# Attention products in plain float32 on tiles of the array, in place of split float32r products

## The chip, the cores and the metric

One Trainium2 chip, one of its cores. The metric is the device time of one launch in microseconds, as the median of several runs. The engines are TensorE (PE in the profile, with PEld for its weight loads), VectorE (DVE), ScalarE (ACT), GpSimd (POOL), and SyncE (SP), which issues nearly all DMA transfers of this kernel. Every engine, and SP's queue, works through its instructions in the order of the program.

## The reference, cut to what matters

Attention over 4 batches and 8 heads of size 64, with 512 local positions and 32 global ones; then two mixture stages on the 2176 tokens, which the change leaves alone.

```python
k_all = np.concatenate([k_g, k_l], axis=2)
v_all = np.concatenate([v_g, v_l], axis=2)
out_g = np.matmul(sm(scale * np.matmul(q_g, k_all.transpose(0, 1, 3, 2))), v_all)
s_ll = scale * np.matmul(q_l, k_l.transpose(0, 1, 3, 2))
s_ll = np.where(np.abs(pos[:, None] - pos[None, :]) <= 32, s_ll, -1000000000.0)
s_lg = scale * np.matmul(q_l, k_g.transpose(0, 1, 3, 2))
a_l = sm(np.concatenate([s_lg, s_ll], axis=-1))
out_l = np.matmul(a_l, np.concatenate([v_g, v_l], axis=2))
x = concatenate([out_g, out_l], axis=2) as 2176 x 512
x = _moe_ref(x, w_in, w_out)                 # relu, square, two products
return _moe2_ref(x, w_gate, w1, w2)          # Sinkhorn gate, 8 experts
```

`sm` is the softmax with 1e-9 added to its sum. A local query thus sees the 32 global keys and the local ones within 32 positions; a global query sees all 544 keys.

## The kernel before, in words

**Attention** comes first. Its work is cut into 16 items, one for each batch and pair of heads (two heads of 64 fill 128 partitions). An item has two local steps of 256 queries each (two tiles of 128 queries, for two heads), and after every second item comes a global step (32 queries of the four heads of two items, 128 rows in all): 40 steps, of which a cycle of five (four local, one global) covers two items. The loop (lines 856 to 927) is a software pipeline written out by hand: in iteration k each engine gets, in this order, the row minimum of step k-1 (`loc_least`, `glob_least`, on DVE; the scores are negated), the normalisation of step k-2 (`loc_normalise`: a reciprocal on DVE, four scalings on POOL), all evacuations that were noted since the last iteration (`evacuate_all`), the exponentials of step k-1 on ACT (`loc_exp`, `glob_exp`), and on TensorE the value products of step k-4 (`loc_values`, `glob_values`), the score products of step k (`loc_scores`, `glob_scores`), the transposes of the probabilities of step k-2 (`loc_transpose`, `glob_transpose`), and at the end of an item the transposes of the keys and queries of a coming item (`prep_qk`).

**Precision.** TensorE's fast form here is float32r, which rounds its operands. Each operand is kept as a half and a rest (hi and lo, both float32r), and each product is made of three: hi times hi, hi times lo, lo times hi (`split_terms`, line 199). So each value that goes from PSUM to SBUF is written twice: ACT casts it to hi (line 552 or 554), and DVE subtracts hi from the PSUM value to get lo (line 557 or 559). That holds for transposed keys (`trk` to `kt`), queries (`trq` to `q`), transposed probabilities (`pta` to `ah`/`al`, `ptb` to `bh`/`bl`), and the outputs (`pv` to `xh`/`xl`, one pair for each head). The values come by DMA to a staging tile, and POOL splits them (`split_pool`, lines 271 and 272).

**Products of a local step.** The scores (line 660) have a contraction of 64: the two heads stand on partitions 0 to 63 and 64 to 127, on two row tiles of the array, and each writes its own score tile: 12 products of 224 columns (128 local keys, 32 global ones, 32 on each side). The values (line 723) use the whole array: the stationary side holds the values of both heads, the moving side the probabilities of both heads (256 columns), so half of the result is not used; 12 products. Keys beside the tile and the global keys lie in the last 96 columns of `kt`, and the values that belong to them in `vb`; both are filled by DMAs inside SBUF (lines 606 to 609, 629 to 633).

**Products of a global step.** For the scores POOL writes the queries of four heads into a tile with zeros elsewhere (`glob_queries`, line 310); 12 products on the whole array (lines 746 and 747, 160 and 384 columns). The values (line 803) are 15 products of 256 columns, a quarter of whose result is used: `pick` takes the four blocks out with two ACT and two DVE instructions.

**What follows.** In the last six iterations the first products of the next stage (line 435) stand between the attention steps; side jobs (`step_side`) prepare its weights on ACT, DVE and POOL, one to three instructions for each iteration, more at the end. From then on order tables written out by hand set the work, and TensorE is kept busy to the end. The gate of the last stage (line 982) already uses plain float32 products, with four column tiles of 32.

Of the kernel before, what the change touches and what calls it, by code (L numbers as in the profile page):

```python
# [9 lines left out]
F32 = mybir.dt.float32  # L10
# [6 lines left out]
WINDOW = 32  # L17
# [188 lines left out]
def kernel(  # L206
# [240 lines left out]
    with ExitStack() as actx:  # L447
# [7 lines left out]
        rawqk, rawv = {}, {}  # L455
# [33 lines left out]
        def load_global(name, src, tag):  # L489
            graw[name] = ap2.tile([P, H * D], F32, tag=tag, name="graw")  # L490
# [7 lines left out]
        load_global("k", k_g, "ah")  # L498
        load_qk(1)
        load_v(0)  # L500
        load_global("v", v_g, "bh")
        load_global("q", q_g, "al")
# [3 lines left out]
        def warm(k):  # L506

            for _ in range(k):
                t = pss.tile([P, 384], F32, tag="pv", name="warm")
                nc.tensor.matmul(t, lhsT=bd[:, 0, 0:P], rhs=bd[:, 0, :], start=True, stop=True)  # L510
# [4 lines left out]
        nc.vector.memset(f32(bd[:, 0]), 0.0)  # L515
        nc.vector.memset(f32(bd[:, 1]), 0.0)
# [15 lines left out]
        for i in range(3):  # L532
            nc.gpsimd.memset(f32(KT[i][:, :, 0, 160:192]), 0.0)
            nc.gpsimd.memset(f32(KT[i][:, :, NQ - 1, 192:224]), 0.0)
            nc.gpsimd.memset(f32(VB[i][32:64, :, 0, :]), 0.0)
            nc.gpsimd.memset(f32(VB[i][64:96, :, NQ - 1, :]), 0.0)
        nc.gpsimd.memset(f32(gz), 0.0)
        for t in OG:
            nc.gpsimd.memset(t, 0.0)

        QT, VA = {}, {}
# [7 lines left out]
        def evacuate_all():  # L549
            for hi, lo, ps, scale in waiting:  # L550
                if scale == 1.0:
                    nc.scalar.copy(hi, ps)
                else:
                    nc.scalar.activation(out=hi, in_=ps, func=AF.Copy, scale=scale)
            for hi, lo, ps, scale in waiting:
                if scale == 1.0:
# [11 lines left out]
        def prep_qk(n):  # L568
# [11 lines left out]
            evacuate((kt[:, 0, :, 0:P], kt[:, 1, :, 0:P], trk, 1.0))  # L580
            if n < 3:
                evacuate((kt[:, 0, 1:, 160:192], kt[:, 1, 1:, 160:192], trk[:, :-1, P - WINDOW : P], 1.0))
                evacuate((kt[:, 0, :-1, 192:224], kt[:, 1, :-1, 192:224], trk[:, 1:, 0:WINDOW], 1.0))
            if n == 0:
                ps = turn_global("k", "pta")
                g = ps[:, p, b * SG : (b + 1) * SG].unsqueeze(1).to_broadcast([P, NQ, SG])
                evacuate((kt[:, 0, :, P : P + SG], kt[:, 1, :, P : P + SG], g, 1.0))
            q = ap2.tile([P, 2, NQ, P], F32R, tag="q", name="q")
            evacuate((q[:, 0], q[:, 1], trq, QSCALE))
            QT[n] = q  # L590
            if n == 0:
                evacuate((kg[:, 0], kg[:, 1], ps, 1.0))

        def prep_edges(n):
# [4 lines left out]
            keys = [f32(kg[:, x, p, b * SG : (b + 1) * SG]).unsqueeze(1).to_broadcast([P, NQ, SG]) for x in range(2)]  # L599
            if n < 3:  # L600
                nc.scalar.copy(kt[:, 0, :, P : P + SG], keys[0])
                nc.vector.tensor_copy(kt[:, 1, :, P : P + SG], keys[1])
# [14 lines left out]
        def prep_v(n):  # L617
# [3 lines left out]
            r = rawv.pop(n)  # L621
            if p % 2 == 0:
                VA[n // 2] = share.tile([P, 2, NQ, 2, P], F32R, tag=f"va{n // 2 % 2}", name="va")
            va = VA[n // 2][:, :, :, p % 2, :]
# [13 lines left out]


        kg = share.tile([P, 2, NP, P], F32R, tag="kg", name="kg")  # L640
        qg = ap1.tile([P, 2, NP, P], F32R, name="qg")
        vg = ap1.tile([P, 2, H * D], F32R, name="vg")
# [6 lines left out]
        def loc_scores(i, n, qp):  # L649
# [44 lines left out]
        def pt_tiles(i, *shapes):  # L694
            pt_t[i] = tuple(
                ap2.tile(shape, F32R, tag=x + y, name=x + y) for x, shape in zip("ab", shapes) for y in "hl"
            )
            return pt_t[i]

        def loc_transpose(i):  # L700
# [9 lines left out]
            ah, al, bh, bl = pt_tiles(i, [P, 2, 2 * P], [96, 2, 2 * P])  # L710
            evacuate((ah, al, pa.rearrange("p t j q -> p t (j q)"), 1.0), (bh, bl, pb[0:96].rearrange("p t j q -> p t (j q)"), 1.0))

        def loc_values(i, n, qp):
            b, p = items[n]
            ah, al, bh, bl = pt_t.pop(i)
            va, vb = VA[n // 2][:, :, :, p % 2, :], VB[n % 3]
            pv = pss.tile([P, 2, 2, P], F32, tag="pv", name="pv")
# [961 lines left out]
```

## Time and profile before

| what | value |
|---|---|
| runs shown | 1962.86, 1963.38, 1964.88 us; median 1963.38 us |
| profiled execution | 1959.21 us, of which the span of instructions is 1957.3 us |
| PE busy | 1928.7 us (99% of the span), 12482 products |
| DVE busy | 1443.9 us (74%) |
| ACT busy | 995.9 us (51%) |
| POOL busy | 581.4 us (30%) |
| mean granted TensorE clock | 0.997 |

A product's duration in the trace includes the time from its start until its last result is written; products follow one another at shorter distances than that, so their cost is read from the starts in the timeline. An engine's busy time in a stretch is the time that at least one of its instructions covers.

### The profile page before, as it was taken

The numbers are of one execution on the slowest core, as the hardware profiler recorded it, in microseconds if no ns is written. First come the engines' busy times: TensorE is split into PE (matmuls) and PEld (weight loads), VectorE is DVE, ScalarE is ACT, GpSimd is POOL, SyncE is SP. The second block draws the span as 40 slices with busy tenths as digits, with TensorE's granted clock in tenths as the row PEclk, the third lists the DMA queues.
The fourth block names the chain that finished last, engine by engine and source line by source line (L and its number), as shares of the span: only waits on it lengthen the run. The fifth ranks groups of instructions, "written<-read, shape, count | busy, mean of one in ns | idle before, by whom it ended". The sixth has DMA issues, their size and how long they took to land.

```text
span 1957.3 us, 34874 instructions
## 1 busy us (share of the span) xinstructions
PE 1928.7 (99%) x12482; PEld 1833.6 (94%) x12482; DVE 1443.9 (74%) x3075; ACT 995.9 (51%) x2325; POOL 581.4 (30%) x673
## 2 busy tenths in 40 slices
PE   9999999999999999999999999999999999999998
PEld 7888988989898899999999999999999999999998
DVE  7998575755359888888886776776777776767867
ACT  7988533323245555545554454454455454554543
POOL 6555431323126554555421101211103101111010
PEclk9999999999999999999999999999999999999999
DMA  7665220211016999998997667667676776676674
GB/s 163 139 144 133 66 65 22 65 44 49 28 32 224 308 302 301 306 301 299 311 329 269 211 224 250 214 237 244 206 260 213 248 249 236 207 258 225 208 267 141
DMA packets 359294, 391.34 MB, mean 200 GB/s; under 512 B 114256, under 2 KB 240208, under 8 KB 359120
## 3 DMA queue, kind: packets, MB, share of 16 engines
q1 hardware_dynamic: 359120, 389.10, 61.1%
q8 instruction: 99, 1.62, 0.3%
q14 instruction: 75, 0.61, 0.1%
HBM read 281.82 MB, written 96.73 MB: 193 GB/s over the span
## 4 chain that ended last, share of the span: by engine, by line
PE 90%; DVE 3%; ACT 2%; DMA 2%; SPq 1%; POOL 1%; issue 1%; DVEq 0%; POOLq 0%; ACTq 0%
PE z L1570 14%; PE a L1331 14%; PE y L1404 11%; PE h L435 10%; PE y L1078 9%; PE d L1570 7%; PE d L1331 7%; PE pa L1331 5%; PE b L1570 4%; PE b L1331 3%; PE pd L1331 2%; PE pb L1331 1%; PE pv L723 1%; ACT e L682 1%; DMA w2forms<-w 1%
## 5 line engine op out<-in xcount | busy, mean ns | idle before, releaser
L1202 POOL TENSOR_TENSOR w<-raw,w 128x256 fp32r<-128x256 f32 (+1 forms) x124 | 122.9, 1023 | 774.0 <-ACT w L1198 697.8
L1331 PE MATMUL a<-xh,w 128*128 128x384 f32 x1024 | 286.0, 335 | 0.0
L1543 ACT CAST xh<-wide 128x384 fp32r<-128x384 f32 x384 | 189.2, 512 | 112.9 <-PE d L1570 95.2
L1547 DVE TENSOR_TENSOR xl<-wide,xh 128x384 fp32r<-128x384 f32 x384 | 200.4, 549 | 24.7 <-ACT xh L1543 24.5
L1532 ACT COPY snaps<-a 128x384 f32<-128x384 f32 x128 | 61.3, 480 | 296.2 <-PE a L1331 224.8
L1404 PE MATMUL y<-w,xh 128*128 128x512 f32 x640 | 197.9, 390 | 0.7 <-ACT xh L1388 0.7
L1078 PE MATMUL y<-hid,w 128*128 128x384 f32 (+1 forms) x960 | 191.7, 356 | 0.0
L1584 DVE SCALAR_TENSOR_TENSOR acc<-z,prob,acc 128x256 f32<-128x256 f32 x366 | 162.0, 475 | 38.8 <-PE z L1570 38.7
L1331 PEld LDWEIGHTS a<-xh,w 128*128 128x128 f32 x1024 | 187.6, 188 | 0.0
L1078 PEld LDWEIGHTS y<-hid,w 128*128 128x128 f32 x960 | 171.9, 188 | 14.9
L435 PE MATMUL h<-xh,w 128*128 128x384 f32 (+1 forms) x640 | 182.6, 358 | 0.0
L1331 PE MATMUL a<-xl,w 128*128 128x384 f32 x512 | 171.2, 334 | 0.0
L1536 DVE TENSOR_TENSOR wide<-b,snaps 128x384 f32<-128x384 f32 x64 | 35.7, 557 | 157.9 <-PE b L1331 156.1
L1331 PE MATMUL d<-xh,w 128*128 128x384 f32 x512 | 150.5, 334 | 0.0
L441 ACT ACTIVATE r<-h 128x384 f32<-128x384 f32 (+1 forms) x76 | 40.4, 532 | 203.3 <-PE h L435 200.4
L1552 DVE TENSOR_TENSOR wide<-wide 128x384 f32<-128x384 f32 x256 | 138.8, 551 | 5.9 <-ACT wide L1540 0.8
L1404 PEld LDWEIGHTS y<-w,xh 128*128 128x128 f32 x640 | 119.2, 188 | 24.8 <-ACT xh L1388 1.1
L435 PEld LDWEIGHTS h<-xh,w 128*128 128x128 f32 x640 | 117.8, 188 | 13.3 <-issue 3.2
L1331 PE MATMUL pa<-xh,w 128*128 128x320 f32 x512 | 128.8, 310 | 1.0 <-ACT snaps L1366 0.6
L1404 PE MATMUL y<-w,xl 128*128 128x512 f32 x320 | 124.7, 390 | 0.9 <-DVE xl L1393 0.9
L1570 PE MATMUL z<-wf,xh 128*128 128x256 f32 x768 | 123.5, 283 | 0.0
L1540 ACT ACTIVATE wide<-wide 128x384 f32<-128x384 f32 x192 | 101.3, 528 | 33.0 <-DVE wide L1536 33.0
(255 smaller groups left out, 5073.4 us busy)
## 6 DMA issues: line engine op xcount, KB each, us to landing
raw<-in_moe_w_dram SPq DMA_DIRECT2D x128, 512.0 KB, 5.7
w<-w1forms SPq DMA_DIRECT2D x256, 256.0 KB, 4.9
w<-w2forms SPq DMA_DIRECT2D x256, 256.0 KB, 5.3
wf<-w2forms SPq DMA_DIRECT2D x192, 256.0 KB, 5.6
w1forms<-w SPq DMA_DIRECT2D x128, 256.0 KB, 4.2
w2forms<-w SPq DMA_DIRECT2D x192, 128.0 KB, 3.2
w2forms<-xl SPq DMA_DIRECT2D x64, 256.0 KB, 4.9
w2forms<-xh SPq DMA_DIRECT2D x64, 256.0 KB, 3.9
```

The lines of the kernel that those rows point to most:

```text
L435: nc.tensor.matmul(ps, lhsT=w, rhs=x, start=(k == 0), stop=(k == 3 * NC - 1))
L1078: nc.tensor.matmul(ps, lhsT=w, rhs=m, start=(f == 0 and x == 0), stop=(f == last and x == 2))
L1202: eng.tensor_tensor(out=lo, in0=src, in1=f32(hi), op=ALU.subtract)
L1331: nc.tensor.matmul(ps, lhsT=lhs, rhs=rhs, start=(first and t == 0), stop=(t == 5), skip_group_check=True)
L1404: nc.tensor.matmul(y[t0], lhsT=lhs, rhs=rhs, start=(t == 0), stop=(t == 3 * UF - 1))
L1532: act.copy(snap[{"1": "p1", "5": "p5" + q, "6": "u2" + q}[i]], bank(("d" if i == "5" else "a") + q)[:, 0:n])
L1540: act.activation(out=dst, in_=bank("a" + q)[:, 0:n] if name == "A21" else dst, func=AF.Relu)
L1543: act.copy(hidden_form(name, 0, int(q)), h[HOME[name]][int(q)])
L1547: dve.tensor_tensor(out=hidden_form(name, 1, q), in0=h[HOME[name]][q], in1=f32(hidden_form(name, 0, q)), op=sub)
L1552: dve.tensor_tensor(out=x, in0=x, in1=h[other][int(q)], op=op)
L1570: nc.tensor.matmul(ps, lhsT=lhs, rhs=rhs, start=(form in ("B11", "T1") and x == 0), stop=(x == 5), skip_group_check=True)
L1584: dve.scalar_tensor_tensor(out=dst, in0=width(t, src), scalar=pr, in1=dst, op0=mul, op1=add)
```

## The change

All products of attention become plain float32 products, each on a part of the array. There is one copy of each operand, no hi and lo. The scores of the two heads stay on two row tiles (four products a step); the values are made for each head on a column tile of 64 (eight products a step); the products of a global step are made for each of four blocks of 32 queries, the scores on a row half and a column tile of 32, the values on a column tile of 32. Evacuations are single copies, given to ACT ("a") or DVE ("v"); only the outputs still have hi and lo, since the next stage takes them so. The values go by DMA straight to `VA`, a ring of eight items, and POOL no longer splits them. `glob_queries` and the block tile `bd` are gone; `pick` is one instruction. `KT`, `VB`, `kg` and `vg` have half the bytes, and lie in the pool of attention rather than in the space shared with later weights. Cut to its core:

```diff
-        KT = [(ap1, share, share)[i].tile([P, 2, NQ, SEG], F32R, tag=f"kt{i}", name=f"kt{i}") for i in range(3)]
-
-        VB = [(ap1, share, share)[i].tile([P, 2, NQ, P], F32R, tag=f"vb{i}", name=f"vb{i}")[0:96] for i in range(3)]
-        bd = ap1.tile([P, 2, 384], F32R, name="bd")
-
-        gz = ap1.tile([P, 2, P], F32R, name="gz")
+        rawqk = {}
+
+        KT = [ap1.tile([P, NQ, SEG], F32, name=f"kt{i}") for i in range(3)]
+        VA = [share.tile([P, 2, NQ, 2, P], F32, tag=f"va{i}", name=f"va{i}") for i in range(2)]
+        VB = [ap1.tile([P, NQ, P], F32, name=f"vb{i}")[0:96] for i in range(3)]
+        kg, qg = (ap1.tile([P, NP, P], F32, name=n) for n in ("kg", "qg"))
+        vg = ap1.tile([P, H * D], F32, name="vg")
+        gz = ap1.tile([P, P], F32, name="gz")
...
+        def values_of(n):
+            return VA[n // 4 % 2][:, n // 2 % 2, :, n % 2, :]
+
         def load_v(n):
             if n >= len(items):
                 return
             b, p = items[n]
-            r = stage.tile([P, 2, NQ, 2, D], F32, tag="r1", name="rv")[:, 0]
-            load_pair(r, v_l, b, p)
-            rawv[n] = r
+            load_pair(values_of(n).rearrange("p t (h d) -> p t h d", h=2), v_l, b, p)
...
+            for eng, hi, lo, ps, scale in waiting:
+                if eng == "a":
+                    if scale == 1.0:
+                        nc.scalar.copy(hi, ps)
+                    else:
+                        nc.scalar.activation(out=hi, in_=ps, func=AF.Copy, scale=scale)
+            for eng, hi, lo, ps, scale in waiting:
+                if lo is not None:
                     nc.vector.tensor_tensor(out=lo, in0=ps, in1=f32(hi), op=ALU.subtract)
-                else:
-                    nc.vector.scalar_tensor_tensor(out=lo, in0=ps, scalar=scale, in1=f32(hi), op0=ALU.mult, op1=ALU.subtract)
+                elif eng == "v":
+                    if scale == 1.0:
+                        nc.vector.tensor_copy(hi, ps)
+                    else:
+                        nc.vector.tensor_scalar(out=hi, in0=ps, scalar1=scale, scalar2=None, op0=ALU.mult)
...
-            evacuate((kt[:, 0, :, 0:P], kt[:, 1, :, 0:P], trk, 1.0))
+            evacuate(("v", kt[:, :, 0:P], None, trk, 1.0))
...
-            q = ap2.tile([P, 2, NQ, P], F32R, tag="q", name="q")
-            evacuate((q[:, 0], q[:, 1], trq, QSCALE))
+                evacuate(("v", kt[:, :, P : P + SG], None, g, 1.0))
+            q = ap2.tile([P, NQ, P], F32, tag="q", name="q")
+            evacuate(("a" if n == 0 else "v", q, None, trq, QSCALE))
...
-                flat = f32(kt).rearrange("p x t k -> p (x t) k")
-                nc.sync.dma_start(out=flat[:, 1:, 160:192], in_=flat[:, :-1, P - WINDOW : P])
-                nc.sync.dma_start(out=flat[:, :-1, 192:224], in_=flat[:, 1:, 0:WINDOW])
-                for x in range(2):
-                    nc.sync.dma_start(out=f32(kt[:, x, :, P : P + SG]), in_=keys[x])
+                nc.sync.dma_start(out=kt[:, 1:, 160:192], in_=kt[:, :-1, P - WINDOW : P])
+                nc.sync.dma_start(out=kt[:, :-1, 192:224], in_=kt[:, 1:, 0:WINDOW])
+                nc.sync.dma_start(out=kt[:, :, P : P + SG], in_=keys)
...
-            split_pool(va[:, 0], va[:, 1], r.rearrange("p t h d -> p t (h d)"))
-            vb = VB[n % 3]
-
-            src, dst = (f32(x).rearrange("p x t d -> p (x t) d") for x in (va, vb))
-            nc.sync.dma_start(out=dst[32:64, 1:], in_=src[P - WINDOW : P, :-1])
-            nc.sync.dma_start(out=dst[64:96, :-1], in_=src[0:WINDOW, 1:])
-            for x in range(2):
-                g = vg[b * SG : (b + 1) * SG, x, p * P : (p + 1) * P]
-                nc.sync.dma_start(out=f32(vb[0:SG, x]), in_=f32(g).unsqueeze(1).to_broadcast([SG, NQ, P]))
+            va, vb = values_of(n), VB[n % 3]
+            nc.sync.dma_start(out=vb[32:64, 1:], in_=va[P - WINDOW : P, :-1])
+            nc.sync.dma_start(out=vb[64:96, :-1], in_=va[0:WINDOW, 1:])
+            g = vg[b * SG : (b + 1) * SG, p * P : (p + 1) * P]
+            nc.sync.dma_start(out=vb[0:SG], in_=g.unsqueeze(1).to_broadcast([SG, NQ, P]))
...
-                pairs = [split_terms(q[r, 0, qt], q[r, 1, qt], kt[r, 0, qt], kt[r, 1, qt]) for r in halves]
-                for x in range(3):
-                    for s, terms in zip(s_t[i], pairs):
-                        a, c = terms[x]
-                        nc.tensor.matmul(s[:, t, :], lhsT=a, rhs=c, start=(x == 0), stop=(x == 2))
+                for s, r in zip(s_t[i], halves):
+                    nc.tensor.matmul(s[:, t, :], lhsT=q[r, qt], rhs=kt[r, qt], start=True, stop=True)
...
-            ah, al, bh, bl = pt_tiles(i, [P, 2, 2 * P], [96, 2, 2 * P])
-            evacuate((ah, al, pa.rearrange("p t j q -> p t (j q)"), 1.0), (bh, bl, pb[0:96].rearrange("p t j q -> p t (j q)"), 1.0))
+            a, c = pt_tiles(i, [P, 2, 2, P], [96, 2, 2, P])
+            evacuate(("a", a, None, pa, 1.0), ("v", c, None, pb[0:96], 1.0))
...
-                terms = split_terms(va[:, 0, qt], va[:, 1, qt], ah[:, t], al[:, t])
-                terms += split_terms(vb[:, 0, qt], vb[:, 1, qt], bh[:, t], bl[:, t])
-                for x, (a, c) in enumerate(terms):
-                    nc.tensor.matmul(pv[:, t].rearrange("p j q -> p (j q)"), lhsT=a, rhs=c, start=(x == 0), stop=(x == 5))
+                for x, (v, e) in enumerate(zip(sources, pt)):
+                    for j, r in enumerate(halves):
+                        nc.tensor.matmul(pv[r, t], lhsT=v[:, qt, r], rhs=e[:, t, j], start=(x == 0), stop=(x == 1))
             c0 = b * SL + qp * 2 * P
-            part = lambda x, r: x[r, p, c0 : c0 + 2 * P].rearrange("p (t q) -> p t q", t=2)
-            evacuate(*((part(xh, r), part(xl, r), pv[r, :, j, :], 1.0) for j, r in enumerate(halves)))
-
-
-        def glob_queries(n):
-            b, p = items[n]
-            v = bd.rearrange("p x (i c) -> p x i c", c=192)
-            for j in range(2):
-                r = slice(j * D, (j + 1) * D)
-                for x in range(2):
-                    copy_pool(v[r, x, :, j * SG : (j + 1) * SG], f32(qg[r, x, p - 1 : p + 1, b * SG : (b + 1) * SG]))
+            part = lambda x: x[:, p, c0 : c0 + 2 * P].rearrange("p (t q) -> p t q", t=2)
+            evacuate(("a", part(xh), part(xl), pv, 1.0))
...
-            for x in range(2):
-                kt = KT[(n - 1 + x) % 3]
-                for y, (a, c) in enumerate(split_terms(bd[:, 0], bd[:, 1], kt[:, 0], kt[:, 1])):
-                    w = a[:, x * P : (x + 1) * P]
-                    first, last = (x == 0 and y == 0), (x == 1 and y == 2)
-                    nc.tensor.matmul(sa, lhsT=w, rhs=c[:, 0, 0 : P + SG], start=first, stop=last)
-                    nc.tensor.matmul(sb, lhsT=w, rhs=c[:, 1:NQ, 0:P], start=first, stop=last)
+            for x, (out, cols) in enumerate(((sa, lambda k: k[:, 0, 0 : P + SG]), (sb, lambda k: k[:, 1:NQ, 0:P]))):
+                for j, r in enumerate(halves):
+                    for y in range(2):
+                        g = slice((2 * j + y) * SG, (2 * j + y + 1) * SG)
+                        w = qg[r, p - 1 + y, b * SG : (b + 1) * SG]
+                        nc.tensor.matmul(out[g], lhsT=w, rhs=cols(KT[(n - 1 + y) % 3][r]), start=True, stop=True)
...
+            (a,) = pt_tiles(i, [P, NQ, P])
+            evacuate(("a", a, None, pa, 1.0), ("v", gz[r], None, pb[r], 1.0))
...
-            for c in range(NQ):
-                terms += split_terms(ah[:, c], al[:, c], va[:, 0, c], va[:, 1, c])
-            terms += split_terms(gz[:, 0], gz[:, 1], v[:, 0], v[:, 1])
-            for y, (a, m) in enumerate(terms):
-                nc.tensor.matmul(pv.rearrange("p h d -> p (h d)"), lhsT=a, rhs=m, start=(y == 0), stop=(y == len(terms) - 1))
+            pv = pss.tile([P, D], F32, tag="pv", name="pv")
+            for c in range(NQ + 1):
+                for j, r in enumerate(halves):
+                    for y in range(2):
+                        g = slice((2 * j + y) * SG, (2 * j + y + 1) * SG)
+                        if c < NQ:
+                            w, v = e[:, c, g], values_of(n - 1 + y)[:, c, r]
+                        else:
+                            w, v = gz[:, g], vg[:, (p - 1 + y) * P + j * D : (p - 1 + y) * P + (j + 1) * D]
+                        nc.tensor.matmul(pv[g], lhsT=w, rhs=v, start=(c == 0), stop=(c == NQ))
             own = OG[n // 2 % 2]
 
             def pick():
-                for h in range(4):
-                    r = slice(h * SG, (h + 1) * SG)
-                    dst = own[r, h % 2 * D : (h % 2 + 1) * D]
-                    if h < 2:
-                        nc.scalar.activation(out=dst, in_=pv[r, h, :], func=AF.Copy, scale=inv[r, 0:1])
-                    else:
-                        nc.vector.tensor_scalar(out=dst, in0=pv[r, h, :], scalar1=inv[r, 0:1], scalar2=None, op0=ALU.mult)
+                src = pv.unsqueeze(1).to_broadcast([P, 2, D])
+                nc.vector.tensor_scalar(
+                    out=own.rearrange("p (j d) -> p j d", j=2), in0=src, scalar1=inv[:, 0:1], scalar2=None, op0=ALU.mult
+                )
...
-                evacuate(*((part(xh, r), part(xl, r), ps[r, :, j, :], 1.0) for j, r in enumerate(halves)))
+                evacuate(*(("a", part(xh, r), part(xl, r), ps[r, j], 1.0) for j, r in enumerate(halves)))
...
-                evacuate((qg[:, 0], qg[:, 1], turn_global("q", "ptb"), QSCALE))
-                split_pool(vg[:, 0], vg[:, 1], graw["v"])
+                evacuate(("v", qg, None, turn_global("q", "ptb"), QSCALE))
             if second:
                 prep_v(n)
-                if n % 2:
-                    glob_queries(n)
```

## Rows read from the trace of the kernel before

**Rows 1.** Stretches: PE, PEld, DVE, ACT, POOL busy (instructions), granted clock, DMA share, GB/s.

```profile
105.64:150.54 44.90, 41.39 (x358) 37.05 (x356) 40.91 (x139) 41.03 (x136) 27.32 (x51) 1.00 0.67 142
...
176.00:181.00 5.00, 3.34 (x22) 2.59 (x22) 3.89 (x12) 3.70 (x13) 4.66 (x11) 1.00 0.12 27
181.00:186.00 5.00, 4.73 (x23) 4.32 (x24) 4.87 (x13) 3.49 (x12) 2.53 (x6) 0.66 0.79 246
...
195.00:203.00 8.00, 8.00 (x45) 6.84 (x44) 2.92 (x7) 3.66 (x8) 2.57 (x2) 1.00 0.00 0
```

**Rows 2.** Timeline of TensorE over one local and one global step: start, length, instructions.

```profile
150.54 0.48 PE L803 MATMUL pv<-va,ah 128*128 128x256 f32 x2
...
152.48 1.00 PE L660 MATMUL s<-kt,q 64*128 64x224 f32 x12
153.41 0.78 PE L706 MATMUL pta<-ident,e 128*128 128x128 f32 x4
...
154.45 0.36 PE L723 MATMUL pv<-ah,va 128*128 128x256 f32 x1
...
155.84 0.28 PE L723 MATMUL pv<-bh,vb 96*128 96x256 f32 x1
156.56 0.34 PE L746 MATMUL s<-kt,bd 128*128 128x160 f32 x1 [0.44 <-POOL bd L310]
...
158.39 0.65 PE L706 MATMUL pta<-ident,e 128*128 128x128 f32 x4
...
160.32 0.36 PE L723 MATMUL pv<-ah,va 128*128 128x256 f32 x1
```

**Rows 3.** Costliest groups on DVE, 105.64 to 150.54 (two cycles): busy, mean ns.

```profile
L557 DVE TENSOR_TENSOR al<-pta,ah 128x512 fp32r<-128x512 f32 x10 | 6.9, 692 | 0.3
L557 DVE TENSOR_TENSOR xl<-pv,xh 64x256 fp32r<-64x256 f32 x16 | 6.7, 419 | 0.3 <-ACT xh L552 0.2
L557 DVE TENSOR_TENSOR bl<-ptb,bh 96x512 fp32r<-96x512 f32 x8 | 5.4, 677 | 0.0
...
L557 DVE TENSOR_TENSOR kt<-trk,kt 128x512 fp32r<-128x512 f32 x4 | 2.8, 692 | 0.1
```

**Rows 4.** The same view and stretch for ACT.

```profile
L552 ACT CAST xh<-pv 64x256 fp32r<-64x256 f32 x17 | 6.1, 360 | 0.1
...
L552 ACT CAST bh<-ptb 96x512 fp32r<-96x512 f32 x8 | 4.7, 585 | 0.0
L554 ACT ACTIVATE q<-trq 128x512 fp32r<-128x512 f32 x4 | 2.4, 604 | 0.0
```

**Rows 5.** The same view and stretch for POOL.

```profile
L272 POOL TENSOR_TENSOR va<-rv,va 128x512 fp32r<-128x512 f32 x4 | 5.7, 1430 | 0.3
```

**Rows 6.** Timeline of TensorE about the plain products of the later gate.

```profile
580.26 0.31 PE L1331 MATMUL pb<-xh,w 128*128 128x320 f32 x1
580.50 0.85 PE L982 MATMUL lt<-acc,gt 128*32 128x384 f32 x8
581.28 0.42 PE L1331 MATMUL pa<-xh,w 128*128 128x320 f32 x1
```

**Rows 7.** Stretches of 0.04 us, line 982 alone: PE, PEld busy (instructions under way).

```profile
580.52:580.56 0.04, 0.04 (x4) 0.04 (x8) 1.00 0.66 205
...
580.84:580.88 0.04, 0.04 (x8) 0.00 (x0) 1.00 0.00 0
```

**Rows 8.** Timeline of SP's queue: start, length, DMAs issued.

```profile
118.49 1.27 SPq L633 DMA_DIRECT2D vb<-vg  x2
119.81 1.16 SPq L467 DMA_DIRECT2D rv<-in_v_l_dram  x2
...
122.48 1.35 SPq L609 DMA_DIRECT2D kt<-kg  x2
```

**Rows 9.** Who waited for whom, 20 to 180: us in total, times, longest.

```profile
PE pv L723 <- DMA vb<-vg: 3.1, 5, 1.4
...
PE s L746 <- POOL bd L310: 2.4, 3, 1.0
```

More of the change, by code (lines that the diff above doesn't have):

```diff
@@ L482, in load_v @@
             b, p = items[n]
-            r = stage.tile([P, 2, NQ, 2, D], F32, tag="r1", name="rv")[:, 0]
-            load_pair(r, v_l, b, p)
-            rawv[n] = r
+            load_pair(values_of(n).rearrange("p t (h d) -> p t h d", h=2), v_l, b, p)
         graw = {}
         def load_global(name, src, tag):
-            graw[name] = ap2.tile([P, H * D], F32, tag=tag, name="graw")
+            graw[name] = ap2.tile([P, H * D], F32, tag=tag, name="graw") if tag else vg
             for b in range(B):
@@ L497 @@
         load_qk(0)
-        load_global("k", k_g, "ah")
+        load_global("k", k_g, "pa")
         load_qk(1)
         load_v(0)
-        load_global("v", v_g, "bh")
-        load_global("q", q_g, "al")
+        load_global("v", v_g, None)
+        load_global("q", q_g, "pb")
         load_qk(2)
@@ L509, in warm @@
                 t = pss.tile([P, 384], F32, tag="pv", name="warm")
-                nc.tensor.matmul(t, lhsT=bd[:, 0, 0:P], rhs=bd[:, 0, :], start=True, stop=True)
+                nc.tensor.matmul(t, lhsT=xh[:, 0, 0:P], rhs=xh[:, 0, 0:384], start=True, stop=True)
         table = ap3.tile([P, 8], F32, tag="st", name="table")
@@ L514 @@
         nc.scalar.activation(out=table, in_=table, func=AF.Copy)
-        nc.vector.memset(f32(bd[:, 0]), 0.0)
-        nc.vector.memset(f32(bd[:, 1]), 0.0)
+        nc.vector.memset(f32(xh[:, 0, 0:384]), 0.0)
         warm(9)
@@ L532 @@
         for i in range(3):
[L533 to L541, printed above, removed]
+            nc.gpsimd.memset(KT[i][:, 0, 160:192], 0.0)
+            nc.gpsimd.memset(KT[i][:, NQ - 1, 192:224], 0.0)
+            nc.gpsimd.memset(VB[i][32:64, 0, :], 0.0)
+            nc.gpsimd.memset(VB[i][64:96, NQ - 1, :], 0.0)
+        nc.gpsimd.memset(gz, 0.0)
+        QT = {}
         waiting = []
@@ L598, in prep_edges @@
             kt = KT[n % 3]
-            keys = [f32(kg[:, x, p, b * SG : (b + 1) * SG]).unsqueeze(1).to_broadcast([P, NQ, SG]) for x in range(2)]
+            keys = kg[:, p, b * SG : (b + 1) * SG].unsqueeze(1).to_broadcast([P, NQ, SG])
             if n < 3:
-                nc.scalar.copy(kt[:, 0, :, P : P + SG], keys[0])
-                nc.vector.tensor_copy(kt[:, 1, :, P : P + SG], keys[1])
-            else:
-                flat = f32(kt).rearrange("p x t k -> p (x t) k")
-                nc.sync.dma_start(out=flat[:, 1:, 160:192], in_=flat[:, :-1, P - WINDOW : P])
-                nc.sync.dma_start(out=flat[:, :-1, 192:224], in_=flat[:, 1:, 0:WINDOW])
-                for x in range(2):
-                    nc.sync.dma_start(out=f32(kt[:, x, :, P : P + SG]), in_=keys[x])
+                nc.scalar.copy(kt[:, :, P : P + SG], keys)
+            else:
+                nc.sync.dma_start(out=kt[:, 1:, 160:192], in_=kt[:, :-1, P - WINDOW : P])
+                nc.sync.dma_start(out=kt[:, :-1, 192:224], in_=kt[:, 1:, 0:WINDOW])
+                nc.sync.dma_start(out=kt[:, :, P : P + SG], in_=keys)
                 if n in EARLY_PARTS:
@@ L637, in prep_v @@
                 load_part(n - len(items) + 3, 1)
-        kg = share.tile([P, 2, NP, P], F32R, tag="kg", name="kg")
-        qg = ap1.tile([P, 2, NP, P], F32R, name="qg")
-        vg = ap1.tile([P, 2, H * D], F32R, name="vg")
         halves = (slice(0, D), slice(D, 2 * D))
@@ L694, in pt_tiles @@
         def pt_tiles(i, *shapes):
-            pt_t[i] = tuple(
-                ap2.tile(shape, F32R, tag=x + y, name=x + y) for x, shape in zip("ab", shapes) for y in "hl"
-            )
+            pt_t[i] = tuple(ap2.tile(shape, F32, tag="p" + x, name="p" + x) for x, shape in zip("ab", shapes))
             return pt_t[i]
@@ L791, in glob_values @@
             b, p = items[n]
-            ah, al = pt_t.pop(i)
+            (e,) = pt_t.pop(i)
             inv = inv_t.pop(i)
-            va = VA[n // 2].rearrange("p x t i d -> p x t (i d)")
-            v = vg[:, :, (p - 1) * P : (p + 1) * P]
-            pv = pss.tile([P, 4, D], F32, tag="pv", name="pv")
-            terms = ()
-            for c in range(NQ):
-                terms += split_terms(ah[:, c], al[:, c], va[:, 0, c], va[:, 1, c])
-            terms += split_terms(gz[:, 0], gz[:, 1], v[:, 0], v[:, 1])
@@ L815, in turn @@
+                nc.vector.tensor_scalar(
+                    out=own.rearrange("p (j d) -> p j d", j=2), in0=src, scalar1=inv[:, 0:1], scalar2=None, op0=ALU.mult
+                )
             def turn():
                 ps = pss.tile([P, 2, 2, SG], F32, tag="pv", name="pv")
-                nc.tensor.transpose(ps.rearrange("p i j q -> p (i j q)"), own, ident)
+                nc.tensor.transpose(ps.rearrange("p j i q -> p (j i q)"), own, ident)
                 c0 = GL + b * SG
                 part = lambda x, r: x[r, p - 1 : p + 1, c0 : c0 + SG]
-                evacuate(*((part(xh, r), part(xl, r), ps[r, :, j, :], 1.0) for j, r in enumerate(halves)))
+                evacuate(*(("a", part(xh, r), part(xl, r), ps[r, j], 1.0) for j, r in enumerate(halves)))
@@ L842, in hidden_early @@
                     yield from hidden_products(g, ps, b * 512, 512)
-                    t = ap2.tile([P, 2, 512], F32, tag="q", name="rs")
+                    t = ap2.tile([P, 2, 512], F32, tag="rs", name="rs")
                     hidden_out(2 * g + b, ps, 512, t[:, 0], t[:, 1], nc.gpsimd)
```

29 lines of the change are left out of this document (7 added, 22 removed).

## The prediction

> **What bounds the kernel now.** I read the stretches first, to find where attention lies and which engine is full there; then the timeline of TensorE, the groups of DVE, ACT and POOL, the plain products that the kernel already has, SP's queue and the waits. The reader should see in the stretches that no engine of attention is alone: from 105.64 to 150.54, two cycles of five steps, PE is covered for 41.4 of 44.9 us, DVE for 40.9 and ACT for 41.0, POOL for 27.3 [rows 1]. Once attention is over (195 to 203), PE is covered throughout and DVE and ACT are under half full [rows 1]. So what attention gains stays gained as long as the weights of the next stage are ready; a cycle of 22.45 us is the thing to shorten.
>
> PE's cover includes the tails of its products, so its own need is read from starts [rows 2]. Local step: values 1.51 us (154.45 to 155.84, and 0.12 for the last one), scores 0.93, eight transposes 0.91 (17 transposes fill 158.39 to 160.32, 0.114 each). Global step: scores 1.83, values 1.94, five transposes 0.57, one for the turn 0.11. Two items need 16 transposes of keys and queries, 1.82. A cycle: 4 x 3.35 + 4.45 + 1.82 = 19.7 us, 88% of its 22.45. DVE and ACT are at 20.5 each, 91%. Three engines near full, each in order, wait for one another now and then; the cycle is 1.14 times PE's need.
>
> **The price of a plain product** is in this trace, on column tiles, in the gate. Line 982 is four products of 384 columns, and the trace has eight instructions: a plain float32 product is two passes. They stand on four column tiles. In the short stretches four are under way together by 580.56, and the second four begin about 0.33 us after the first [rows 7]: so a pass costs 0.86 ns a column, and the four tiles overlap fully. From the first start (580.50) to the next product (581.28) is 0.78 us, 0.12 more than two passes [rows 6]; I charge this 0.12 to each block of products on tiles, as the cost of changing the array's shape.
>
> **PE after, by cycle.** Local scores: four products, two passes each, two heads side by side: 4 x 224 x 0.86 ns + 0.12 = 0.89 us (0.93 now). That two row tiles overlap is seen today: at the values' pace (0.12 us for 256 columns) 12 products of 224 columns would need 1.26 us one by one, and they take 0.93 [rows 2]. Local values: eight products of 128 columns, two halves side by side: 8 x 0.11 + 0.12 = 1.00 (1.51 now). Transposes stay, 0.91. Four local steps: 11.2. Global scores: two passes of 160 and two of 384 columns, four tiles side by side: 0.94 + 0.12 = 1.06 (1.83 now). Global values: 20 products, 40 passes of 64 columns, four side by side: 0.55 + 0.12 = 0.67 if columns set it. No row shows a long run of passes so short. Below, the bound is this 0.67, since four column tiles cannot do better than overlap fully; above, the 0.07 a product of today's score block [rows 2], 40 x 0.07 = 2.8. The nearest row, with the same tiles, starts four passes and eight weight loads within 0.06 us [rows 7], so I take 0.8. With 0.57, 0.11 and 1.82 as before the sum is 11.2 + 1.06 + 0.8 + 2.5 = 15.6 us, against 19.7.
>
> For the global scores the row shows four tiles that take all 128 rows each [rows 6]; here two of the four use the upper half of the rows and two the lower, and all write one PSUM bank. The Trainium skill ("TensorEngine Tiling (Array Packing)", Gotcha 1: PSUM Pressure) says that different row tiles cannot access the same bank at the same time. By the row this block is 1.06 us; by that page the two halves would take turns, which is a rival below.
>
> **DVE, by cycle.** Out of two cycles' 40.9 us: all of `al` goes (6.9), half of `xl` (one instruction on all partitions for two on half of them, 3.35 of 6.7) [rows 3]. `bl` becomes a copy of 96 x 512 from PSUM, and `kt` and `q` become copies of 128 x 512; the trace has no such copy on DVE. It lies between 0.42 us (half as many columns, `xl`) and the 0.69 of the subtraction with a second operand [rows 3]; I take 0.6, near the latter, as the columns are the same. That saves 0.6 on `bl` and 0.7 on keys and queries. `pick` is one instruction for two, not counted. 40.9 - 11.6 = 29.3, or 14.7 a cycle. What queues behind the copies is the row minimum of the next step; it gets to run earlier, as the engine has less in front of it.
>
> **ACT**: `bh` goes (4.7), `q` (2.4) and as much again for `kt`, half of `xh` (3.05) [rows 4]: 41.0 - 12.5 = 28.5, 14.3 a cycle. **POOL** loses the subtraction of the split, 5.7 in two cycles [rows 5], its copy and the block queries besides, and was never the bound. The waits for its block queries (2.4 us in 160) and for the values' last DMA (3.1) [rows 9] lose their cause: the values are in place two items ahead.
>
> **SP's queue.** Per item it loses one `vb` issue and one `kt` issue, about 0.65 us each [rows 8], and has the same loads otherwise. They wait for nothing new: a value load goes to a slot whose readers ended many steps ago. The DMAs of key edges now wait for DVE's copy in place of DVE's subtraction, which stood at the same point. The start (fewer clears, no split of the global values before the first normalisation) I cost at nothing: the loads and the first exponentials hide it.
>
> **The sum.** PE stays the fullest engine (15.6, with 14.7 and 14.3 beside it), so I keep the ratio of today: 15.6 x 1.14 = 17.8 us a cycle, 4.65 less. From 20 to 176 us there are 156 / 22.45 = 6.95 cycles: 32.3 us. The value blocks among the first products of the next stage are worth about 2 more, some of it lost to side jobs. In all 34.5 us. The profiled execution, 1959.2, would become 1924.7; against the median of 1963.4, which is 4.2 us above it, I predict 1929. Its own range: with a ratio of 1.05 and the global values at 0.67 a cycle is 16.2 us, a gain of 46 (1917); with those values at 2.8 it is 20.1, a gain of 17 (1946).
>
> **Rivals.** (1) *The passes do not overlap*, the slower one. Each plain product is two passes on the same tile, one right after the other in the program; if the second holds up the product on the other tile, the halves run one by one. Against it: line 982 has this order in its code, and overlaps [rows 7]. For it: no row has passes on two row tiles, or 16 in a row. Then a local step is 8 x 0.193 + 16 x 0.11 + 0.24 + 0.91 = 4.45, a global one 3.86 + 2.32 + 0.68, a cycle 26.5; one full engine waits little, say 1.05: 27.8 us. 5.35 x 6.95 and 3 for the rest give +40: 2003. It decides once a cycle's PE time passes 22.45 / 1.05 = 21.4, when about half of the pairs run alone.
>
> (2) *The clock.* From 176 to 181 PE was covered for only 3.3 of 5 us, and in the next 5 us the granted clock was 0.66, part of the time at 1.2 instead of 2.4 GHz [rows 1]. If the new steps leave PE looking as idle, at half clock a cycle is 31.1 x 1.05 = 32.7 us, up to +71 (2034); it turns the sign above a share of 0.31 of attention. Against it: PE stays the fullest engine in my sum.
>
> (3) *One bank at a time.* The global scores double to 2.0 us, a cycle is 16.5 x 1.14 = 18.8 us, and the gain 27: 1936. That is the result by the page's rule; no run yet shows it.
>
> (4) *The side jobs set the end of attention.* Between 176 and 181 POOL is full (4.7 of 5) and PE is not [rows 1]. If the weights of the next stage pace the last cycle and the tail, their 4.65 and 2 are not gained: about 28, 1935.
>
> **How the numbers follow.** Forecast 0.68, (1) 0.08, (2) 0.08, (3) 0.07, (4) 0.09. About 0.2%, 4 us, is what can be told from no change. The forecast, (3) and (4) are all faster, 0.84; (1) and (2) are slower but for mild forms of them, which may land near zero: slower 0.14, same 0.02. The range holds the forecast's own ends with (3) and (4), 1914 to 1950, and leaves out the two slower cases.
>
> **What would show it.** Each plain product as two passes, 0.19 us apart in the scores with both heads under way together; value blocks near 1.0 us and score blocks near 0.9; global values under 1 us; `al`, `bl`, `bh` and the split on POOL gone; a cycle, from one global value block to the next, near 17.8 us; attention over some 35 us earlier, and the stretch behind it as full as before. A cycle over 22 us, passes that start one after another, or a granted clock under 0.9 in attention would make the prediction wrong.

## The result, and the profile after

The changed kernel takes 1933.5 us (median of four runs, 1929.2 to 1938.8) beside 1963.8 for the kernel before: a ratio of 0.9847, interval 0.9821 to 0.9872. That is 30 us less, where 34.5 were forecast, and inside the range. But the way there differs from the working: TensorE's blocks cost nearly what the sum said, two of seven cycles are shorter than the 17.8 us that it gave, and five are longer, up to 22.2.

The first view is the start of the page of the changed kernel; its profiled execution took 1938.8 us, the slowest of the four.

```profile
span 1937.0 us, 34930 instructions
...
PE 1907.6 (98%) x12714; PEld 1794.2 (93%) x12714; DVE 1398.1 (72%) x2984; ACT 947.6 (49%) x2204; POOL 541.3 (28%) x605
```

PE has 232 more matmul instructions than before (a plain product counts as two), and 21 us less of busy time; DVE and ACT lost 46 and 48 us.

Next, TensorE's timeline of the changed kernel over a global value block, a local step and a global score block (start, length, instructions), to be read beside [rows 2].

```profile
115.45 0.65 PE L772 MATMUL pv<-va,pa 128*32 128x64 f32 x32
115.93 0.29 PE L772 MATMUL pv<-vg,gz 128*32 128x64 f32 x8
116.15 1.03 PE L642 MATMUL s<-kt,q 64*128 64x224 f32 x8
117.11 0.44 PE L686 MATMUL pta<-ident,e 128*128 128x128 f32 x2
...
118.96 0.44 PE L702 MATMUL pv<-pa,va 128*64 128x128 f32 x4
119.23 0.39 PE L702 MATMUL pv<-pb,vb 96*64 96x128 f32 x4
...
119.99 1.12 PE L716 MATMUL s<-kt,qg 64*32 64x160 f32 x16
121.04 0.66 PE L686 MATMUL pta<-ident,e 128*128 128x128 f32 x4
```

From start to next start: 40 passes of the global values in 0.70 us (forecast 0.8, before 1.94), scores 0.96 (0.89), local values 1.03 (1.00, before 1.51), global scores 1.05 (1.06, before 1.83). The passes overlap in pairs and in fours, on row tiles too: at 0.86 ns a column the 16 passes of the global scores would take some 3.7 us one after the other (an estimate).

Four cycles of the changed kernel, each from one global value block to the next (columns as in [rows 1]):

```profile
36.86:53.20 16.34, 16.34 (x207) 12.93 (x206) 13.83 (x58) 13.78 (x52) 6.97 (x16) 1.00 0.61 130
53.20:74.90 21.70, 18.14 (x208) 14.17 (x207) 14.35 (x59) 14.45 (x53) 7.11 (x17) 0.92 0.53 117
74.90:93.24 18.34, 17.17 (x207) 12.99 (x206) 16.11 (x61) 14.31 (x53) 10.78 (x18) 1.00 0.63 135
93.24:115.45 22.21, 19.18 (x207) 15.07 (x206) 14.33 (x59) 14.54 (x53) 7.16 (x17) 0.85 0.53 116
```

The first cycle is 16.34 us, and PE is covered from end to end: it alone sets the time. I call such a cycle undisturbed. The second and the last are almost as long as those of before (22.45), and the granted clock is below one in them. The third lies between; PE is idle for 1.17 us of it, at full clock. Next, TensorE's timeline in the last of the four shows why.

```profile
102.49 0.60 PE L689 MATMUL ptb<-ident,e 128*96 128x128 f32 x4
103.02 0.44 PE L702 MATMUL pv<-pa,va 128*64 128x128 f32 x4
106.48 0.70 PE L702 MATMUL pv<-pb,vb 96*64 96x128 f32 x4 [3.02 <-DMA vb<-vg]
...
107.96 1.87 PE L642 MATMUL s<-kt,q 64*128 64x224 f32 x8
109.76 1.11 PE L750 MATMUL pta<-ident,e 128*128 128x128 f32 x4
```

In the middle of a value block PE waits 3.02 us for the global values in `vb`. Behind it a score block takes 1.80 us where 0.96 is usual. The stretches of the two parts, and the waits of PE from 20 to 150 us (total, times, longest):

```profile
102.00:107.00 5.00, 1.98 (x20) 1.58 (x20) 2.48 (x12) 3.20 (x11) 0.00 (x0) 0.83 0.61 137
107.00:112.00 5.00, 5.00 (x29) 4.06 (x26) 2.00 (x11) 1.46 (x5) 1.03 (x3) 0.50 0.32 58
```

```profile
PE pv L702 <- DMA vb<-vg: 9.0, 4, 3.6
PE s L642 <- DVE st L653: 0.9, 2, 0.7
```

After the wait the granted clock is 0.50, so 1.2 instead of 2.4 GHz, for some 5 us. The cycle's excess over 16.34 is 5.87 us: 3.02 of waiting and 2.85 of slow products (PE is covered for 19.18 us of it). All waits on `vb` come to 9.0 us, where the kernel before had 3.1 in a longer stretch [rows 9]: 2.0 at 22 us, when attention starts, 3.6 at 67, 3.0 here and 0.3 later.

SP's queue before that wait (start, length, DMAs):

```profile
96.92 0.57 SPq L363 DMA_DIRECT2D raw<-in_moe_w_out_dram  x1
100.11 0.93 SPq L467 DMA_DIRECT2D rqk<-in_k_l_dram  x2
101.09 1.82 SPq L467 DMA_DIRECT2D rqk<-in_q_l_dram  x2
102.95 0.65 SPq L620 DMA_DIRECT2D vb<-va  x1
103.65 0.64 SPq L621 DMA_DIRECT2D vb<-va  x1
104.34 0.60 SPq L623 DMA_DIRECT2D vb<-vg  x1
```

At item 10 an early weight piece (line 363) is staged in the same two-buffer ring as keys and queries. The load that comes next needs the buffer of an item whose transposes are only now made, so the queue stands still from 97.5 to 100.1; the DMAs into `vb` are behind it. The last of those transposes on TensorE:

```profile
99.81 0.27 PE L580 MATMUL trq<-ident,rqk 128*128 128x128 f32 x1
```

The kernel before has the same order, and its queue stood still at the same place, from 110.9 to 115.0; PE then waited 0.8 us for `vb`. SP's queue there, and what SP's queue waited for these transposes from 20 to 180 us (total, times, longest), first before and then after:

```profile
110.28 0.57 SPq L363 DMA_DIRECT2D raw<-in_moe_w_out_dram  x1
114.99 0.92 SPq L467 DMA_DIRECT2D rqk<-in_k_l_dram  x2
```

```profile
SPq L467 <- PE trq L578: 9.9, 5, 4.1
SPq L467 <- PE trq L580: 13.3, 5, 4.2
```

On DVE and ACT the copies have come in place of casts and subtractions; three of DVE's costliest groups, 20 to 150 us:

```profile
L559 DVE COPY pb<-ptb 96x512 f32<-96x512 f32 x27 | 18.3, 678 | 0.9 <-PE ptb L689 0.8
L556 DVE TENSOR_TENSOR xl<-pv,xh 128x256 fp32r<-128x256 f32 x27 | 11.3, 419 | 0.2 <-ACT xh L551 0.2
L559 DVE COPY kt<-trk 128x512 f32<-128x512 f32 x13 | 8.9, 688 | 0.5
```

A copy out of PSUM takes DVE 0.68 us, as long as the subtraction with a second operand did [rows 3].

### The profile page after: what moved, and what is told of

Same layout as the page of the kernel before. It is cut to its first block, busy times and chain, and to the rows that moved or that the text cites. A ratio compares the mean times of both kernels' runs of the same rounds, so it can differ in the third digit from the quotient of the medians.

```text
span 1937.0 us, 34930 instructions
## 1 busy us (share of the span) xinstructions
PE 1907.6 (98%) x12714; PEld 1794.2 (93%) x12714; DVE 1398.1 (72%) x2984; ACT 947.6 (49%) x2204; POOL 541.3 (28%) x605
## 4 chain that ended last, share of the span: by engine, by line
PE 92%; DMA 3%; DVE 2%; SPq 1%; POOL 1%; issue 0%; ACT 0%; DVEq 0%; POOLq 0%
PE z L1533 13%; PE a L1294 13%; PE y L1367 11%; PE h L435 10%; PE y L1041 10%; PE d L1533 7%; PE d L1294 6%; PE pa L1294 5%; PE b L1533 3%; PE b L1294 3%; PE pd L1294 2%; PE pv L702 1%; PE pb L1294 1%; PE s L642 1%; DMA w<-w2forms 1%; PE pta L686 1%
## 5 line engine op out<-in xcount | busy, mean ns | idle before, releaser
L1510 DVE TENSOR_TENSOR xl<-wide,xh 128x384 fp32r<-128x384 f32 x384 | 200.8, 550 | 24.9 <-ACT xh L1506 24.6
```

Of the source, the lines that this page charges most:

```text
L1510: dve.tensor_tensor(out=hidden_form(name, 1, q), in0=h[HOME[name]][q], in1=f32(hidden_form(name, 0, q)), op=sub)
```

## The experiments

The theory after this result: PE's need sets the cycle at 16.3 us, and what the sum lacked is SP's queue, which delivers `vb` late at a few places; each delay costs its wait and, for the most part, a stretch at half clock. Rivals: the transfers are slow in themselves; or PE does not set the cycle at all, and the relief of DVE and ACT brought the gain alone.

### The changed kernel again

No edit; the level for the three runs after it.

> The changed kernel once more, as the level for the runs beside it. Four runs gave 1929.2 to 1938.8 us, a spread of 0.5% where the kernel before has 0.1%. If the stalls of TensorE on the DMAs into vb (3.6 and 3.0 us in the profile, each followed by a stretch at half clock) depend on when transfers land, the spread should show again, 1929 to 1939, and the stalls be of other lengths in this profile; if they are set by the order of SP's queue alone, they should stand at the same two places again.

1934.3 us (1930.4 to 1935.2; ratio 0.9853, 0.9838 to 0.9868). Its cycles are 16.3, 19.0, 17.6, 21.7, 17.5, 19.4 and 19.5 us, and the two long waits inside the cycles stand at the same two places, after items 6 and 10, with other lengths:

```profile
66.03 0.44 PE L702 MATMUL pv<-pb,vb 96*64 96x128 f32 x4 [2.32 <-DMA vb<-vg]
...
103.84 0.44 PE L702 MATMUL pv<-pb,vb 96*64 96x128 f32 x4 [3.54 <-DMA vb<-vg]
```

So the order of the queue sets the place. The landing of the transfers does not set the length: in all four long waits PE went on 2.1 to 2.5 us after the last of the three DMAs had been issued; what differs is how far PE had come by then. A third wait, 2.0 and 2.3 us, stands at 22 us in both profiles. Behind the wait at 66.03 the granted clock stayed at 1.00, so a stretch at half clock does not follow every wait. The spread of the times goes with all that, though no run shows that it is the whole of it.

### Early pieces in another ring

```diff
-                    load_part(0, EARLY_PARTS[n], tag="r0")
+                    load_part(0, EARLY_PARTS[n], tag="r1")
```

> One word: the two early weight pieces (items 6 and 10) are staged in the ring that the values no longer use, not in the two-buffer ring of keys and queries. Theory: a piece in that ring makes the next load of keys and queries wait in SP's queue for transposes that are only just made, and the DMAs into vb queue behind it. Then the two stalls (64 and 103 us) go, with the half clock behind each: 6.6 us of waiting and about 4 us of slow products, so 8 to 11 us less, 1922 to 1926. Rival: the vb transfers are slow in themselves, through many small packets. Then the stalls stay and the time is that of the changed kernel, 1929 to 1939.

1924.3 us (1922.5 to 1925.2; ratio 0.9805, 0.979 to 0.982), 10 us less than the run beside it. In SP's queue at item 10 the load follows the weight piece at once:

```profile
91.94 0.62 SPq L363 DMA_DIRECT2D raw<-in_moe_w_out_dram  x1
92.67 0.93 SPq L467 DMA_DIRECT2D rqk<-in_k_l_dram  x2
...
97.03 0.60 SPq L623 DMA_DIRECT2D vb<-vg  x1
```

The wait at item 10 shrank from 3.5 to 0.2 us and its cycle from 21.7 to 16.8; all waits on `vb` fell from 8.7 to 3.6, and SP's waits for the transposes, 10.5 us in the run beside it, are gone. One word in the code was worth a third of what the whole change had brought, and at item 10 the theory of the queue holds. But it said that both stalls would go, and the one at item 6 stayed (2.3, now 2.2); this time the granted clock fell behind it (0.92 over the cycle, 1.00 in the run beside it), and the cycle grew from 19.0 to 20.3 us. There the queue no longer stands still, it is full: the piece's 512 KB, the loads and the `vb` DMAs follow one another without a gap, and the last of these DMAs took 3.1 us to land, where it took 2.1 in the run beside it. So the rival, slow transfers, has a part in this wait. Another 3.0 us of the gain lie in the sixth cycle (19.4, now 16.3) and 1.7 ahead of the first; what links them to the ring was not followed up.

### Local values on the whole array

```diff
-                    for j, r in enumerate(halves):
-                        nc.tensor.matmul(pv[r, t], lhsT=v[:, qt, r], rhs=e[:, t, j], start=(x == 0), stop=(x == 1))
+                    nc.tensor.matmul(
+                        pv[:, t].rearrange("p j q -> p (j q)"), lhsT=v[:, qt, :], rhs=e[:, t].rearrange("p j q -> p (j q)"),
+                        start=(x == 0), stop=(x == 1),
+                    )
```

> One part undone: the local values stay plain float32, but on the whole array, both heads in 256 columns, 8 passes instead of 16 on column tiles; two output evacuations on each of ACT and DVE instead of one. Theory (TensorE is the fullest engine): a value block grows from 1.03 to 8 x 0.22 = 1.76 us, 0.73 more for 64 steps less 32... that is 32 local steps, 23 us more, or 18 to 25 with some of it in the stalls: 1951 to 1958. Rival: the waits set the cycle, TensorE has room, and the time moves by under 8 us.

(cut to the products; the outputs are again evacuated by two instructions on each of ACT and DVE instead of one)

1947.2 us (ratio 0.9922, 0.9907 to 0.9937), 13 more than the changed kernel beside it: below the theory's range, above the rival's. The block itself grew as expected; TensorE's timeline has 1.83 us from 60.41 to 62.24:

```profile
60.41 0.60 PE L701 MATMUL pv<-pa,va 128*128 128x256 f32 x2
60.85 0.60 PE L701 MATMUL pv<-pb,vb 96*128 96x256 f32 x2
...
62.24 1.12 PE L718 MATMUL s<-kt,qg 64*32 64x160 f32 x16
```

That is 0.80 more, 3.2 a cycle, and more than the 1.51 of the split products before: on the whole array plain products would have made this block slower, the tiles make it faster. The short cycles are 18.4 to 20.0 us instead of 16.3 to 17.6. But the seven cycles from the first global value block to the last took 146.0 us against 131.0, 15 more and not 22: with slower steps `vb` comes in time more often (waits of 5.6 us for 8.7). PE sets the undisturbed cycle (in the first of the seven it is covered for all of 19.16 us); a cost on PE is partly paid out of the stalls.

### The subtractions back on DVE

```diff
             for eng, hi, lo, ps, scale in waiting:
+                if lo is None and hi.shape[0] >= 96 and len(hi.shape) == 4:
+                    junk = ap2.tile([P, 2, 2, P], F32, tag="junk", name="junk")[0 : hi.shape[0]]
+                    nc.vector.tensor_tensor(out=junk, in0=ps, in1=ident[0 : hi.shape[0]].unsqueeze(1).unsqueeze(1).to_broadcast([hi.shape[0], 2, 2, P]), op=ALU.subtract)
```

> One relief undone: DVE gets two subtractions of 512 columns back in each local step (into a tile that nothing reads), as many as the kernel before had for the probabilities. Products as in the changed kernel. DVE's need rises by 4 x 1.37 = 5.5 us a cycle, from about 15 to 20.5, above TensorE's 15.6. Theory (the products alone could not have brought the gain, DVE stood at its limit too): a cycle is 20.5 to 22 us and most of the gain goes, 25 to 35 us more, 1955 to 1966. Rival (the gain is TensorE's, DVE had room): under 8 us more.

1943.4 us (ratio 0.9906, 0.989 to 0.9923): 9 more, again between the two. The seven cycles are 18.4 to 21.5 us, 20.2 on average. One of them, with the columns of [rows 1], shows DVE covered for 20.17 of 21.21 us, and PE for 17.21:

```profile
117.03:138.24 21.21, 17.21 (x222) 12.86 (x215) 20.17 (x70) 14.49 (x53) 9.65 (x20) 1.00 0.55 117
```

DVE's load, 18.9 us a cycle on average, is a little under that of before (20.2). With it the new products bring about three fifths of the cycles' gain: from 22.4 us on average to 20.2, where the changed kernel beside it has 18.7; the waits on `vb` are alike (8.5 and 8.7 us). The shortest cycle, 18.4 instead of 16.3, says nearly the same.

### The copies all on ACT

```diff
-            evacuate(("v", kt[:, :, 0:P], None, trk, 1.0))
+            evacuate(("a", kt[:, :, 0:P], None, trk, 1.0))
...
-            evacuate(("a" if n == 0 else "v", q, None, trq, QSCALE))
+            evacuate(("a", q, None, trq, QSCALE))
...
-            evacuate(("a", a, None, pa, 1.0), ("v", c, None, pb[0:96], 1.0))
+            evacuate(("a", a, None, pa, 1.0), ("a", c, None, pb[0:96], 1.0))
```

> The other relief undone, on the changed kernel: the copies of transposed probabilities, keys and queries all go to ACT, as the casts did before, and DVE has none of them. ACT's need goes from about 14 to 14.3 + 4 x 0.59 + 4 x 0.59 = 19 us a cycle, DVE's falls by 4.9; products as in the changed kernel. Theory (a cycle needs all three engines relieved, the fullest sets it): cycles of 19 to 20.5 us and, as with the load on DVE, 6 to 12 us more than the 1934 beside which it ran, since the stalls on vb are partly covered: 1940 to 1946. Rival (TensorE alone sets the cycle): within 3 us of 1934.

1937.7 us (1936.5 to 1938.6; ratio 0.9871, 0.9854 to 0.9887), 3.5 more than the changed kernel's 1934.3 (the kernel before took 1962.5 beside this run and 1962.2 beside that one): a miss, little beyond the rival's 3. The cycles show the mechanism all the same: none is below 18.6 us, and PE now waits for the exponentials on ACT before each score block that follows a global step.

```profile
PE s L642 <- ACT e L732: 6.1, 6, 1.1
PE pv L702 <- DMA vb<-vg: 3.4, 2, 2.1
```

The waits on `vb` fell from 8.7 to 3.4 us meanwhile, so most of what ACT takes comes out of the stalls.

### The DMAs into `vb` one step earlier

```diff
+            if first and n > 1:
+                edges_v(n)
             if k in (1, 3) or first and n > 1:
                 prep_edges(n + 1)
```

(cut; `edges_v` holds the three DMAs that `prep_v` had, and `prep_v` keeps them for items 0 and 1; on top of the other ring)

> The ring kernel (1924.3 us) with the three DMAs into vb put one step earlier in SP's queue, ahead of the key edges and the loads of coming items, from item 2 on. Theory (what is left of the waits, 0.9 + 0.4 + 2.2 + 0.2 us in its profile, is the place in SP's queue): the waits at 46, 65 and 100 us go, with the stretch at half clock behind the second; 3 to 6 us less, 1918 to 1921. Rival (the transfer itself is late, for the traffic beside it): no change, 1922 to 1926.

1924.9 us (1924.2 to 1926.5): no change against the 1924.3 of the ring alone, so the theory as I put it missed. The rival gave this time, but not this profile; the waits moved:

```profile
PE s L644 <- DMA kt<-kg: 3.1, 4, 1.5
...
PE pv L704 <- DMA vb<-vg: 1.2, 1, 1.2
```

Now the key edges, which are behind `vb`, come late. So it is not the place in the queue alone; that the queue as a whole is the second limit is what the next run asks.

### The DMAs into `vb` on POOL's queue

```diff
-            nc.sync.dma_start(out=vb[32:64, 1:], in_=va[P - WINDOW : P, :-1])
+            nc.gpsimd.dma_start(out=vb[32:64, 1:], in_=va[P - WINDOW : P, :-1])
```

(and the other two alike, on top of the other ring, in their old place)

> The ring kernel (1924.3 us) with the three DMAs into vb of each item issued from POOL's queue in place of SP's, at the same point of the program. With the DMAs one step earlier in SP's queue the waits only moved from vb to the key edges (3.6 to 3.1 us). Theory: SP's queue is the second limit, some 7 us of issues for an item that now takes about 7 us of steps; freed of 1.9 us an item, neither vb nor kt is waited for, cycles come down to 16.3 to 17, and the time to 1917 to 1921. Rival: the transfers land late whoever issues them, or POOL's issues hold up its scalings; then waits on vb or on POOL stay or grow, 1923 to 1930.

1921.8 us (1921.1 to 1922.0; ratio 0.9794, 0.9781 to 0.9808), the fastest version, between the theory's range and the rival's. Its interval overlaps that of the ring alone; its five runs all lie below the other's four. PE's list of waits from 20 to 150 us is this one line, and no DMA is in it:

```profile
PE pta L686 <- POOL e L674: 2.5, 5, 1.1
```

Four of its seven cycles are 16.5 or 16.6 us, two 18.0 and 18.2, and the last, with the side jobs, 20.7. So what was left of the DMA waits went with SP's queue, but little time hung on them. Without them the first six cycles are 2.7 us shorter in all than with the ring alone; the last is 2.2 longer, at a granted clock of 0.84 where the ring's had 1.00. In the two cycles of 18 us POOL, which now issues these DMAs as well, is covered for 14.3 us instead of 10.8.

## Why the prediction was right, and where it was not

**The price of plain products**: right. Two passes of 0.86 ns a column, tiles side by side, 0.12 us for the change of shape: the four kinds of block came out within 0.1 us. The transposes, left at 0.91 us a local step, took 0.93 to 1.03, and all of PE's work in the undisturbed cycle adds up to 16.34 us, not 15.6.

**One bank at a time** (rival 3): not so here. The four tiles of a global score block, two on either half of the rows, write one bank (that of the 160 columns first, then that of the 384). Four passes are under way together 0.1 us after the block's start at 40.57, and the block takes 1.05 us; 2.0 was the price by the rule. The Trainium skill ("TensorEngine Tiling (Array Packing)", Gotcha 1: PSUM Pressure) says that different row tiles cannot use one bank at the same time. Here the tiles write different partitions of it, and the measurement decides.

**PE stays the fullest engine**: right. An undisturbed cycle has PE covered from end to end (16.34 of 16.34 us), with DVE and ACT at 13.8. The loads put back on PE, DVE and ACT each lengthened the shortest cycle. DVE's copies took 0.68 us and not 0.6; DVE had room for that.

**The ratio of 1.14**, taken over from before, is the term that failed. It stood for engines that wait for one another a little everywhere. Without stalls the ratio is 16.34 / 15.6 = 1.05, the good end of the range, and even this is no waiting but the 0.7 us by which the sum was short. Over seven cycles of the first profiled execution, from 36.86 to 173.09 us, the mean is 19.5, or 1.25, and 18.7 or 1.20 in the second. In the first, PE is idle for 11.6 us of the seven cycles, 6.9 of them for `vb`, and covered for 10 us more than in seven undisturbed ones, most of it in the four cycles with a granted clock of 0.84 to 0.92.

**SP's queue** is the step behind that failure. I wrote that the loads "wait for nothing new" and that the wait for `vb` loses its cause, because the values are there two items ahead. The values' load is early indeed. But the queue is in order: the early weight piece holds one of two buffers of keys and queries, the next load waits for transposes, and the three `vb` DMAs stand behind. This stop was not new, it was left out: in the kernel before, SP's queue already stood still for 9.9 us on those transposes, and PE waited 3.1 us for `vb` in all [rows 9]. With shorter steps the same queue is late more often. Taking the piece out of that ring gave 10 us, half of it in the cycle of item 10.

**The clock** (rival 2) came in a mild form, not through PE's lighter work but behind most of the long waits: 0.50 for some 5 us after the wait of 3.02. No run separates its share from that of the waits. **The side jobs** (rival 4) kept part of their share: the last cycle, with three side jobs an iteration, is 18.5 to 21 us in the changed kernel and in all three versions of its queue, where it was 23.0 before; the granted clock in it goes from 1.00 in the shortest to 0.84 in the two longest. **Passes one by one** (rival 1) is excluded by the blocks.

**The number** was near partly by luck. An undisturbed cycle that was too long in the sum stood against stalls that were not in it, and the stalls weighed more: the seven cycles are 20.4 and 25.6 us shorter in the two profiles, where 4.65 each would be 32.5. The start, costed at nothing, gave 2.0 and 1.8 us (the first global value block begins at 38.90 us before, at 36.86 and 37.15 after). As a whole the two profiled executions of the changed kernel are 20.4 and 24.6 us shorter than that of the kernel before. The medians are 30 and 28 us apart, because the one profiled execution of before lies 3.0 to 4.6 us under its medians and the first of the changed kernel 5.3 over its own; no trace shows why the one of before was that fast.

## What to carry to other kernels

Where a product is made three times from halves and rests only for precision, plain products on parts of the array can cost less (here 1.03 us for a value block instead of 1.51, where the whole array took 1.83), and the single copies relieve every engine that empties PSUM. When a pipeline gets faster, walk its in-order DMA queue again, item by item, with the new step length: here it stopped at a buffer shared by two kinds of loads, a stop that the trace of before already showed. And while such stalls exist, an engine experiment shows too little in the time; read the undisturbed cycle.

## What the runs showed of the hardware that was not expected

Forty passes of 64 columns with weights of 32, four column tiles, take 0.70 us in all, 17.5 ns a pass with the change of shape in it. Four tiles, two on the upper and two on the lower half of the rows, wrote different partitions of one bank at the same time. After a wait of 3.02 us in attention the granted clock fell to 0.50 for about 5 us, so that late DMA cost nearly twice its wait (5.87 us). That is the dearest case: in the second profile the cycle with the wait of 3.54 is 5.35 us above 16.34, and the one with the wait of 2.32, at full clock, 2.64.
